# Turning the attention weights of slots 5 to 8 of the first batch on VectorE and through DRAM instead of on TensorE

## The chip, the cores and the metric

The kernel runs on one core of one Trainium2 chip. The metric is the device time of one execution in microseconds (us). Five engines work beside each other, each through its own instructions in order, and wait for one another by semaphores: TensorE (PE in the profile, with its weight loads PEld), VectorE (DVE), ScalarE (ACT), GpSimd (POOL) and SyncE (SP), whose queue issues nearly all DMAs here.

## The reference

For each of 8 batches and 8 heads, attention with a threshold: only the scores within tau of the row's maximum keep their weight. The heads of a batch are put side by side as x, and a feed-forward block (FFN) with normalisation follows.

```python
def _attn_ref(q, k, v, tau):              # q, k, v: (8, 8, 576, 64)
    scores = scale * np.matmul(q, k.transpose(0, 1, 3, 2))
    thresh = np.max(scores, axis=-1, keepdims=True) - tau
    scores = np.where(scores >= thresh, scores, -1000000000.0)
    scores = scores - np.max(scores, axis=-1, keepdims=True)
    attn = np.exp(scores)
    attn = attn / (np.sum(attn, axis=-1, keepdims=True) + 1e-09)
    return np.matmul(attn, v)

def _moe_ref(x, g_ln, w_ch1, w_ch2):      # x: (8, 576, 512); w_ch1: 512 x 2048, w_ch2: 2048 x 512
    mu = np.mean(x, axis=-1, keepdims=True)
    var = np.mean((x - mu) ** 2, axis=-1, keepdims=True)
    xn = (x - mu) / np.sqrt(var + 1e-06) * g_ln
    ch = np.maximum(xn @ w_ch1, 0.0) @ w_ch2
    return x + ch
```

The two weight matrices arrive as 64-bit floats; the kernel makes 32-bit floats of them on the chip.

## The kernel before

The kernel writes out the order of every engine's instructions by hand: what stands first in the Python code stands first in the engine's queue.

**Slots.** Attention goes through 72 slots, nine to a batch (`SLOTS`, with `HP` = 4 pairs of heads). Slots 0 to 3 take the first 256 queries of a pair of heads each, slot 4 takes the last 64 queries of all pairs together, slots 5 to 8 the second 256 queries. A slot has four quarters. In slot n, `scores` (matmuls on TensorE into PSUM) comes first; `exponentials` makes the negated maxima `neg` on VectorE (L372) and the exponentials `e` on ScalarE (L383); `weights` masks them and sums their rows on VectorE (L390) and takes the reciprocals `den` (L394). The scores of slot n+1 go into the same PSUM tiles, so they wait for L390 of slot n.

**Turning the weights.** For the product with v the weights must stand with the keys on the partitions. There are two ways, chosen by `by_blocks`. In batch 0, slot n+1 does it on TensorE (`turn_weights`): GpSimd makes four diagonal matrices of `den` (L404), and 36 matmuls of 64 columns by 128, that is four tiles `tp` and one tile `tr`, turn and divide at once; ScalarE copies each tile out of PSUM into `em` and `rest` (L437, L452). Two of the four tiles are turned ahead of the exponentials of slot n+1 and the others after the first two of them. In batches 1 to 7 `turn_blocks` does it: GpSimd divides `e` (L404), VectorE transposes blocks of 32x32 into `et` (L469), SP writes `et` to a DRAM buffer `scr` in four DMAs (L475), and in quarter 0 of the next slot `fetch` reads it back as `em` and `rest` in two (L484, L485). `values_of` multiplies with v (L511) in quarter 2 or 3 of slot n+1, ScalarE copies the result into `x`, and GpSimd sums x over its features (L537).

**The feed-forward part.** The 576 tokens of a batch make two groups of 288. When a group's last x is there, `mean_of` forms its mean by a matmul and `centre` subtracts it on VectorE (L552). `ffn_steps` yields 129 steps a group: first 16 tiles `hidden`, four matmul pairs each into one of two PSUM buffers with a relu on ScalarE (L606), and then 4 output tiles of 16 steps. `second_part` deals these steps out over the quarters: `ready(g)` names the quarter from which group g may run, and its steps are spread until `ready(g + 1)`.

**Weight chunks.** `Weights` brings the weights in 32 chunks of 128x512 64-bit numbers (16 of w_ch1, 16 of w_ch2), each into a piece of SBUF that is not yet needed for its own purpose (`w2_sb`, `hidden`, `et`, a tile `stage`). `fetch` issues the DMA on SP (L221), `tick` works on at most three chunks: `begin` (two VectorE and two ScalarE instructions), `carry` (GpSimd L257) one tick later, and `end` (VectorE L266, and GpSimd L271 for w_ch1) three ticks later. Slots 0 to 2 have three ticks each, slots 3 to 5 four, later ones six. A step of the feed-forward part whose weights are not made yet puts the quarter's work off.

Of the kernel before, what the change touches and what calls it, by code (L numbers as in the profile page):

```python
# [8 lines left out]
F32 = mybir.dt.float32  # L9
# [9 lines left out]
def kernel(  # L19
# [140 lines left out]
    class Weights:  # L160
# [12 lines left out]
        def __init__(self):  # L173
            self.chunks = [
                (w1_sb[i][:, c : c + WC], w_ch1[i * 128 : (i + 1) * 128, c : c + WC], i)
                for c in range(0, DF, WC)
                for i in range(NK)
            ] + [(w2_sb[:, i], w_ch2[i * 128 : (i + 1) * 128, :], None) for i in range(ND)]
            self.n1 = NK * (DF // WC)
            self.fetched = self.begun = self.carried = self.ended = 0  # L180
            self.raw, self.made, self.due, self.ticks = {}, {}, [], 2
            flat = lambda t: t.rearrange("p a b -> p (a b)")
            stage = consts.tile([128, 8, WC], F32, name="stage")
            et = att.tile([128, NB, 128], F32, tag="et", bufs=1, name="et0")

            n1 = self.n1
            self.free = []  # L190
            for t, n, before in (
                (w2_sb, ND // 2, lambda p: n1 + 2 * p),
                (hidden, 4, lambda p: 10),
                (et, 2, lambda p: 2 * n1),
                (stage, 4, lambda p: 2 * n1),
            ):
                for p in range(n):
                    self.free.append((before(p), -1, flat(t)[:, p * 2 * WC : (p + 1) * 2 * WC]))
# [84 lines left out]
            if self.begun < self.fetched:  # L283
                self.begin()

    def by_blocks(u):

        return units[u][0] > 0

    def turn(u):  # L290

        q_in, k_in = loaded.pop(u)
        qT = att.tile([128, 2, QH], F32, tag="qT", bufs=4, name="qT")
        kT = att.tile([128, S], F32, tag="kT", bufs=4, name="kT")
        qd = q_diag[u % HP]  # L300
        nc.gpsimd.tensor_scalar(
            out=q_in, in0=q_in, scalar1=scl_sb, scalar2=1.0, op0=ALU.mult, op1=ALU.mult
        )
        nc.vector.transpose(kT, k_in.rearrange("p n c -> p (n c)"))
        for s in range(2):
            part = q_in[:, 9 * s : 9 * s + 8]
            if by_blocks(u):
                nc.vector.transpose(
                    qT[:, s].rearrange("p (j a c) -> p a j c", j=2, a=4),
                    part.rearrange("p (a j) c -> p a j c", j=2),  # L310
                )
            else:
                nc.vector.transpose(qT[:, s], part.rearrange("p n c -> p (n c)"))
        for h in range(2):
            r = slice(64 * h, 64 * h + 64)
            nc.vector.transpose(
                qd[r, r].rearrange("p (t c) -> p t c", t=2),
                q_in[r].rearrange("p (t n) c -> p t n c", t=2)[:, :, 8],
            )
        turned[u] = (qT, kT, qd)  # L320
# [64 lines left out]
    def weights(es, thr, divide):  # L385


        den = small.tile([128, 4], F32, tag="den", name="den")
        for i in range(4):
            nc.vector.scalar_tensor_tensor(  # L390
                out=es[:, i], in0=blocks[i], scalar=thr[:, i : i + 1], in1=es[:, i],
                op0=ALU.is_ge, op1=ALU.mult, accum_out=den[:, i : i + 1],
            )
        nc.vector.reciprocal(den, den)  # L394
        diags = []
        for i in range(4):
            if divide:
                src = dst = es[:, i]
            else:
                if i % 2 == 0:  # L400
                    two = ffn.tile([128, TOK], F32, tag="o", bufs=6, name="diag")
                src, dst = ident, two[:, i % 2 * 128 : i % 2 * 128 + 128]
                diags.append(dst)
            nc.gpsimd.tensor_scalar(  # L404
                out=dst, in0=src, scalar1=den[:, i : i + 1], scalar2=1.0,
                op0=ALU.mult, op1=ALU.mult,
            )
        return diags
# [9 lines left out]
    def turn_weights(s, es, diags):  # L418


        em, er = turned_tiles(s)
        for i in range(4):
            if i == 2:
                yield
            tp = ps_ff.tile([128, J, 128], F32, tag="ff", name="tp")
            for c in range(J):
                product(
                    tp[:, c], lhsT=es[:, i, c * 128 : (c + 1) * 128], rhs=diags[i],
                    start=True, stop=True,
                )  # L430
            if s == HP:
                nc.scalar.copy(
                    em[:, :, :, 32 * i : 32 * i + 32], tp.rearrange("p c (a x) -> p c a x", a=4)
                )
            else:
                h, j = divmod(i, 2)
                nc.scalar.copy(  # L437
                    em[:, :, 2 * j : 2 * j + 2, 64 * h : 64 * h + 64],
                    tp.rearrange("p c (a x) -> p c a x", a=2),
                )  # L440
        tr = ps_ff.tile([64, 4, 128], F32, tag="ff", name="tr")
        for i in range(4):
            nc.tensor.matmul(  # L443
                tr[:, i], lhsT=es[:, i, J * 128 :], rhs=diags[i], start=True, stop=True
            )
        if s == HP:
            nc.scalar.copy(
                er[:64].rearrange("p a (u x) -> p u a x", u=HP),
                tr.rearrange("p u (a x) -> p u a x", a=4),
            )  # L450
        else:
            nc.scalar.copy(  # L452
                er[:64].rearrange("p a (h x) -> p h a x", h=2),
                tr.rearrange("p (h j) (a x) -> p h (j a) x", h=2, a=2),
            )
        yield em, er

    def turn_blocks(s, es):

# [35 lines left out]
    def values_of(b, s, turned_weights):  # L495

        em, er = turned_weights
        pv = pv_behind
        if b == 0 and s <= HP:
            pv = ps_ff.tile([128, QH], F32, tag="ff", name="pv")  # L500
        if s == HP:
            outs = [(hp, pv[:, hp * 64 : hp * 64 + 64]) for hp in range(HP)]
            pick = lambda t, hp, h: t[:, 2 * h : 2 * h + 2, hp * 32 : hp * 32 + 32]
        else:
            outs = [(s if s < HP else s - HP - 1, pv)]
            pick = lambda t, hp, h: t[:, :, 64 * h : 64 * h + 64]
        for hp, dst in outs:
            vt, vr = values_in[b * HP + hp]
            for c in range(J + 1):
                for h in range(2):  # L510
                    nc.tensor.matmul(  # L511
                        dst[64 * h : 64 * h + 64],
                        lhsT=vt[:, c, h, :] if c < J else vr[:, h, :],
                        rhs=pick(em[:, c] if c < J else er, hp, h),
                        start=(c == 0), stop=(c == J),
                    )
        if s == HP:
            for t in range(2):
                nc.scalar.copy(
                    x_of(2 * b + t)[:, :, QH:],  # L520
                    pv.rearrange("p (u t x) -> p t u x", u=HP, t=2)[:, t],
                )
                for c in range(1, NK):
                    add_feature(2 * b + t, c, slice(QH, TOK))
        else:
            g = 2 * b + (s > HP)
            hp = outs[0][0]
            nc.scalar.copy(x_of(g)[:, hp, :QH], pv)  # L528
            if hp:
                add_feature(g, hp, slice(0, QH))  # L530
# [114 lines left out]
    def at_quarter(n, i, fn, *args):  # L645
        later_calls.setdefault((n, i), []).append((fn, args))
# [5 lines left out]
    def ready(g):  # L652

        if g < 2:
            return (24, 41)[g]
        b, t = divmod(g, 2)
        return QUARTERS * (b * SLOTS + (HP, 2 * HP)[t] + 2) + (2, 4)[t]

# [43 lines left out]
    for n in range(NS):  # L702
# [24 lines left out]
        tick(1)  # L727
        run(n, 1)
        second_part(n, 1)
        blocks_go = by_blocks(b * HP)  # L730
        diags = weights(es, thr, blocks_go)
        run_all(aside)
        run_all(stores)
# [5 lines left out]
        if blocks_go:  # L739
            scr = turn_blocks(s, es)  # L740
            at_quarter(n + 1, 0, lambda s=s, scr=scr, box=box: box.append(fetch(s, scr)))
        else:
            made = turn_weights(s, es, diags)
            at_quarter(n + 1, -1, next, made)
            at_quarter(n + 1, 0, lambda made=made, box=box: box.append(next(made)))
        at_quarter(
            n + 1, 2 if b == 0 and s <= HP else 3,
            lambda b=b, s=s, box=box: values_of(b, s, box[0]),
        )
        if s in (HP, 2 * HP):  # L750
# [49 lines left out]
```

## Time and profile before

| | |
|---|---|
| median of 3 runs | 1514.7 us (1514.58 to 1514.93) |
| the profiled execution | 1510.16 us, span 1508.4 us |
| TensorE busy | 1423.0 us, 94% of the span |
| VectorE, ScalarE, GpSimd busy | 55%, 29%, 31% of the span |
| start of the scores of slots 0 to 5 | 9.6, 25.6, 39.6, 54.9, 69.8, 88.9 us |
| start of the scores of slots 6 to 10 | 113.7, 142.1, 170.2, 187.9, 221.1 us |
| first feed-forward matmul | 124.1 us |

The span is what the profiler saw of the kernel's own instructions; the profiled execution took 1.8 us more than it. Times in the timeline count from the span's start. A matmul in 32-bit floats is recorded as two records, and `product` issues two matmuls, so one feed-forward step leaves four records.

### The profile page before, as it was taken

What the parts mean: (1) busy time and instruction counts of PE and PEld (TensorE: products, weight loads), DVE (VectorE), ACT (ScalarE), POOL (GpSimd) and SP (SyncE); (2) the same over time, 40 slices, a digit from 0 to 9 for tenths busy, and PEclk for the clock granted to TensorE, in tenths of its full rate; (3) what the DMA queues carried; (4) which work ended last, traced back from release to release, by engine and by line L of the source; (5) the groups of instructions that cost most, each with busy time, mean ns of one, the idle gap of its engine ahead of it and who ended that gap; (6) DMA issues with size and microseconds to landing.
All of it is one profiled execution on the core that took longest, in us unless ns stands there. A gap on an engine that the chain in (4) does not pass through costs nothing.

```text
span 1508.4 us, 29807 instructions
## 1 busy us (share of the span) xinstructions
PE 1423.0 (94%) x12168; PEld 861.2 (57%) x12168; DVE 822.3 (55%) x1380; ACT 442.6 (29%) x797; POOL 470.5 (31%) x737
## 2 busy tenths in 40 slices
PE   4859999999999999999999999999999999999998
PEld 2647655565556555565556555565555655565554
DVE  5877646555645555455655556455564556455210
ACT  3655513223231322223132322314132232313120
POOL 3785323332323333232322323232232323232100
PEclk8879999999999999999999999999999999999999
DMA  9613146557765577456764577456774568545300
GB/s 226 164 56 107 38 98 140 161 138 163 167 159 132 133 160 173 128 138 153 172 168 120 133 167 175 131 138 155 169 170 129 139 150 185 138 114 132 95 9 16
DMA packets 460696, 205.12 MB, mean 136 GB/s; under 512 B 275024, under 2 KB 420176, under 8 KB 460560
## 3 DMA queue, kind: packets, MB, share of 16 engines
q1 hardware_dynamic: 458160, 202.93, 55.5%
q8 instruction: 95, 1.56, 0.4%
q10 hardware_dynamic: 2368, 0.30, 0.2%
q14 instruction: 41, 0.34, 0.1%
q0 software_dynamic: 32, 0.00, 0.0%
HBM read 119.41 MB, written 83.76 MB: 135 GB/s over the span
## 4 chain that ended last, share of the span: by engine, by line
PE 85%; ACT 6%; DVE 4%; SPq 1%; issue 1%; POOL 1%; DMA 1%; POOLq 0%; ACTq 0%; DVEq 0%
PE p L100 62%; PE sc L511 10%; PE sc L359 9%; ACT e L383 4%; DVE neg L372 2%; PE sc L100 2%; SPq L112 1%; ACT hidden L606 1%; PE tp L100 1%; DMA v_rest<-in_v_dram 1%; POOL diag L404 1%; PE tr L443 1%; ACT L383 1%; PE mean L100 1%; DVE e L390 0%
## 5 line engine op out<-in xcount | busy, mean ns | idle before, releaser
L100 PE MATMUL p<-xc,w 128*64 128x288 f32 x4096 | 520.6, 409 | 24.7 <-ACT hidden L606 24.1
L100 PE MATMUL p<-hidden,w 128*64 128x288 f32 x4096 | 513.6, 407 | 0.2 <-ACT rest L452 0.2
L100 PEld LDWEIGHTS p<-xc,w 128*64 128x64 f32 x4096 | 296.2, 137 | 227.5 <-ACT hidden L606 39.9
L100 PEld LDWEIGHTS p<-hidden,w 128*64 128x64 f32 x4096 | 293.3, 137 | 195.5 <-ACT rest L452 0.7
L372 DVE TENSOR_REDUCE neg<-sc 128x2 f32<-128x1152 f32 x144 | 189.4, 1353 | 343.5 <-PE sc L359 278.6
L383 ACT ACTIVATE e<-sc,neg 128x576 f32<-128x576 f32 x288 | 193.0, 743 | 275.8 <-DVE neg L372 275.6
L404 POOL TENSOR_SCALAR e<-e,den 128x576 f32<-128x576 f32 x252 | 183.6, 746 | 231.3 <-DVE den L394 226.4
L390 DVE SCALAR_TENSOR_TENSOR e<-sc,thr,e 128x576 f32<-128x576 f32 x288 | 219.1, 813 | 20.1 <-ACT e L383 19.4
L469 DVE STREAM_TRANSPOSE et<-e 128x1152 f32<-128x1152 f32 x112 | 153.2, 1372 | 72.8 <-POOL e L404 61.8
L359 PE MATMUL sc<-kT,qT 64*128 64x64 f32 (+3 forms) x1024 | 159.5, 445 | 27.0 <-DVE e L390 16.8
L606 ACT ACTIVATE hidden<-p 128x288 f32<-128x288 f32 x256 | 105.1, 415 | 270.3 <-PE p L100 268.3
L376 POOL TENSOR_SCALAR thr<-neg,low_sb 128x2 f32<-128x2 f32 x144 | 42.1, 293 | 374.6 <-DVE neg L372 371.6
L359 PEld LDWEIGHTS sc<-kT,qT 64*128 64x128 f32 x1024 | 88.8, 194 | 113.2 <-issue 81.5
L511 PE MATMUL sc<-em,v_in 128*64 128x256 f32 (+1 forms) x1408 | 130.8, 329 | 1.8 <-DVE o L569 1.8
L528 ACT COPY x<-sc 128x256 f32<-128x256 f32 x60 | 22.4, 373 | 321.5 <-PE sc L511 321.5
L511 PEld LDWEIGHTS sc<-em,v_in 128*64 128x64 f32 x1408 | 86.1, 137 | 40.3 <-DVE o L569 2.3
L569 DVE TENSOR_TENSOR o<-p,rb 128x288 f32<-128x288 f32 x64 | 28.4, 444 | 127.0 <-PE p L100 127.0
L570 POOL TENSOR_TENSOR o<-o,x 128x288 f32<-128x288 f32 x64 | 51.1, 798 | 137.3 <-DVE o L569 135.8
L537 POOL TENSOR_TENSOR sum<-sum,x 128x256 f32<-128x256 f32 (+1 forms) x64 | 31.4, 491 | 100.4 <-ACT x L528 97.9
L612 POOL TENSOR_TENSOR sq<-sq 128x288 f32<-128x288 f32 x48 | 39.0, 813 | 50.4 <-ACT sq L610 47.9
L618 DVE RECIPROCAL rb<-rb 128x288 f32<-128x288 f32 x16 | 31.2, 1950 | 35.3 <-ACT rb L617 35.0
L511 PE MATMUL sc<-rest,v_rest 128*64 128x256 f32 (+1 forms) x352 | 44.5, 329 | 0.0
(109 smaller groups left out, 741.2 us busy)
## 6 DMA issues: line engine op xcount, KB each, us to landing
scr<-et SPq DMA_DIRECT2D x252, 288.0 KB, 4.8
em<-scr SPq DMA_DIRECT2D x63, 1024.0 KB, 5.9
q_in<-in_q_dram SPq DMA_DIRECT2D x128, 72.0 KB, 3.7
out_dram<-ot SPq DMA_DIRECT2D x256, 36.0 KB, 4.1
k_in<-in_k_dram SPq DMA_DIRECT2D x124, 72.0 KB, 2.6
v_in<-in_v_dram SPq DMA_DIRECT2D x64, 128.0 KB, 4.1
rest<-scr SPq DMA_DIRECT2D x63, 128.0 KB, 6.0
w<-in_moe_w_ch_dram SPq DMA_DIRECT2D x12, 512.0 KB, 4.9
```

Source lines behind the costliest of these rows:

```text
L100: nc.tensor.matmul(out[r], lhsT=lhsT[:, r], rhs=rhs, **flags)
L359: nc.tensor.matmul(sc[h][:, at : at + n], lhsT=qT[r, half, j * 128 : (j + 1) * 128], rhs=kT[r, o : o + n], start=True, stop=True,)
L372: nc.vector.tensor_reduce(out=neg[:, i], in_=sc[h][:, : 2 * S].rearrange("p (j n) -> p j n", j=2), axis=AXL.X, op=ALU.max, negate=True,)
L376: nc.gpsimd.tensor_scalar(out=thr[:, i], in0=neg[:, i], scalar1=-1.0, scalar2=low_sb, op0=ALU.mult, op1=ALU.add,)
L383: nc.scalar.activation(es[:, i], blocks[i], func=AF.Exp, bias=neg[:, i : i + 1])
L390: nc.vector.scalar_tensor_tensor(out=es[:, i], in0=blocks[i], scalar=thr[:, i : i + 1], in1=es[:, i], op0=ALU.is_ge, op1=ALU.mult, accum_o ...
L404: nc.gpsimd.tensor_scalar(out=dst, in0=src, scalar1=den[:, i : i + 1], scalar2=1.0, op0=ALU.mult, op1=ALU.mult,)
L469: nc.vector.transpose(et[:, :, 64 * h : 64 * h + 64].rearrange("p n (j c) -> p j n c", j=2), es[:, 2 * h : 2 * h + 2].rearrange("p j (n c) ...
L511: nc.tensor.matmul(dst[64 * h : 64 * h + 64], lhsT=vt[:, c, h, :] if c < J else vr[:, h, :], rhs=pick(em[:, c] if c < J else er, hp, h), s ...
L570: nc.gpsimd.tensor_tensor(out=o, in0=o, in1=groups[g][:, m], op=ALU.add)
L606: nc.scalar.activation(hidden[:, d], p1, func=AF.Relu)
L612: nc.gpsimd.tensor_tensor(out=sq[:, 0], in0=sq[:, 0], in1=sq[:, c], op=ALU.add)
```

## The change

Five edits go together.

1. `by_blocks` now depends on the slot: in batch 0, slots 5 to 8 go by blocks and DRAM as all slots of later batches do. Their queries are transposed accordingly in `turn`.
2. The diagonals that are left (slots 0 to 4) are made by ScalarE, not by GpSimd.
3. `turn_weights` is no longer cut in two: all five tiles are turned ahead of the exponentials of slot n+1.
4. `ready` of the first two groups moves by a quarter. The mean of group 0 goes from the end of slot 5 to quarter 0 of slot 6, behind that slot's scores; the first feed-forward steps go from quarter 0 to quarter 1 of slot 6.
5. Pieces for chunks: those in `hidden` serve longer (up to chunk 15 to 18, before up to 9), those in `et` shorter (up to chunk 15, before to the end), and one tile `x_room` of the pool of x comes in.

```diff
@@ class Weights
             for t, n, before in (
                 (w2_sb, ND // 2, lambda p: n1 + 2 * p),
-                (hidden, 4, lambda p: 10),
-                (et, 2, lambda p: 2 * n1),
+                (hidden, 4, lambda p: n1 + p),
+                (et, 2, lambda p: n1),
+                (ffn.tile([128, NK, TOK], F32, tag="x", bufs=3, name="x_room"), 1, lambda p: 2 * n1),
                 (stage, 4, lambda p: 2 * n1),
             ):
@@
-    def by_blocks(u):
-
-        return units[u][0] > 0
+    def by_blocks(b, s):
+
+        return b > 0 or s > HP
@@ turn
-            if by_blocks(u):
+            if by_blocks(units[u][0], 2 * HP * s):
@@ weights
         for i in range(4):
-            if divide:
-                src = dst = es[:, i]
-            else:
+            if not divide:
                 if i % 2 == 0:
                     two = ffn.tile([128, TOK], F32, tag="o", bufs=6, name="diag")
-                src, dst = ident, two[:, i % 2 * 128 : i % 2 * 128 + 128]
-                diags.append(dst)
+                diags.append(two[:, i % 2 * 128 : i % 2 * 128 + 128])
+                nc.scalar.mul(diags[i], ident, den[:, i : i + 1])
+                continue
             nc.gpsimd.tensor_scalar(
-                out=dst, in0=src, scalar1=den[:, i : i + 1], scalar2=1.0,
+                out=es[:, i], in0=es[:, i], scalar1=den[:, i : i + 1], scalar2=1.0,
                 op0=ALU.mult, op1=ALU.mult,
             )
@@ turn_weights
         for i in range(4):
-            if i == 2:
-                yield
             tp = ps_ff.tile([128, J, 128], F32, tag="ff", name="tp")
...
-        yield em, er
+        return em, er
@@ values_of
-        if b == 0 and s <= HP:
+        if not by_blocks(b, s):
             pv = ps_ff.tile([128, QH], F32, tag="ff", name="pv")
@@ ready
         if g < 2:
-            return (24, 41)[g]
+            return (25, 42)[g]
@@ the loop over slots
-        blocks_go = by_blocks(b * HP)
+        blocks_go = by_blocks(b, s)
         diags = weights(es, thr, blocks_go)
...
         else:
-            made = turn_weights(s, es, diags)
-            at_quarter(n + 1, -1, next, made)
-            at_quarter(n + 1, 0, lambda made=made, box=box: box.append(next(made)))
+            at_quarter(
+                n + 1, -1,
+                lambda s=s, es=es, diags=diags, box=box: box.append(turn_weights(s, es, diags)),
+            )
         at_quarter(
-            n + 1, 2 if b == 0 and s <= HP else 3,
+            n + 1, 3 if blocks_go else 2,
             lambda b=b, s=s, box=box: values_of(b, s, box[0]),
         )
```

## The prediction

> **What bounds the kernel now.** I began with the page's forty slices of the span:
>
> ```profile
> PE   4859999999999999999999999999999999999998
> POOL 3785323332323333232322323232232323232100
> PEclk8879999999999999999999999999999999999999
> ```
>
> TensorE is full from the fourth slice (113 us) on; the idle time is ahead of it. Busy time slot by slot is the next view (columns: length, then busy time of PE, PEld, DVE, ACT, POOL; clock; DMA share; GB/s):
>
> ```profile
> 69.80:88.90 19.10, 13.65 (x127) 10.23 (x123) 15.61 (x29) 12.24 (x22) 14.71 (x15) 0.82 0.20 71
> 88.90:113.60 24.70, 13.21 (x173) 10.87 (x172) 17.09 (x29) 14.23 (x27) 21.84 (x28) 0.77 0.15 47
> 113.60:142.10 28.50, 25.81 (x238) 21.71 (x237) 24.51 (x35) 13.29 (x24) 15.54 (x16) 0.96 0.24 80
> 142.10:170.20 28.10, 25.74 (x241) 16.87 (x240) 17.17 (x27) 16.43 (x29) 9.05 (x11) 1.00 0.25 81
> 187.90:221.10 33.20, 29.96 (x274) 18.75 (x274) 12.69 (x24) 5.84 (x10) 8.02 (x12) 1.00 0.36 74
> 221.10:239.90 18.80, 18.80 (x156) 10.96 (x154) 12.49 (x24) 5.71 (x10) 7.33 (x11) 1.00 0.56 122
> ```
>
> Slots 4 and 5 are bound by a chain over VectorE, GpSimd and ScalarE; from slot 6 on TensorE sets the length, and what it is spared there shortens the run. Its timeline from slot 5 to slot 7 and in slot 9 (start, length, work, idle time before it):
>
> ```profile
> 112.49 1.23 PE L100 MATMUL mean<-sum,avg_sb 128*64 128x288 f32 x4 [6.33 <-POOL sum L537]
> 113.65 3.38 PE L359 MATMUL sc<-kT,qT 64*128 64x512 f32 x16
> 116.96 3.75 PE L100 MATMUL tp<-diag,e 128*64 128x128 f32 x64
> 123.40 0.98 PE L443 MATMUL tr<-diag,e 128*64 128x128 f32 x7 [2.69 <-ACT em L437]
> ...
> 124.33 12.29 PE L100 MATMUL p<-xc,w 128*64 128x288 f32 x99
> ...
> 144.35 3.89 PE L100 MATMUL tp<-diag,e 128*64 128x128 f32 x64
> 148.76 0.98 PE L443 MATMUL tr<-diag,e 128*64 128x128 f32 x7 [0.51 <-ACT em L437]
> ```
>
> The mean holds up the scores of slot 6 for 6.33 us, and each turn stands in front of feed-forward work. In the waits of slots 2 to 5 and in VectorE's timeline GpSimd is what is late: the diagonals, four in 3.5 us, stand ahead of the chunk work that VectorE needs next.
>
> ```profile
> 89.00 3.51 POOL L404 TENSOR_SCALAR diag<-ident,den 128x128 f32<-128x128 f32 x4 [2.44 <-PE pv L511]
> ```
> ```profile
> 50.06 0.77 DVE L313 STREAM_TRANSPOSE qT<-q_in 128x256 f32<-128x256 f32 x2 [2.15 <-POOL q_in L301]
> 77.34 1.20 DVE L266 SCALAR_TENSOR_TENSOR hidden<-hidden 128x512 f32<-128x512 f32 x1 [2.20 <-POOL hidden L257]
> 94.48 1.20 DVE L266 SCALAR_TENSOR_TENSOR et<-et 128x512 f32<-128x512 f32 x1 [2.20 <-POOL et L257]
> ```
>
> And the DMA prices (KB each, us from issue to landing):
>
> ```profile
> scr<-et SPq DMA_DIRECT2D x252, 288.0 KB, 4.8
> em<-scr SPq DMA_DIRECT2D x63, 1024.0 KB, 5.9
> w<-in_moe_w_ch_dram SPq DMA_DIRECT2D x12, 512.0 KB, 4.9
> ```
>
> **What the Trainium skill says.** "SBUF — State Buffer", section "SBUF: two separate sides": VectorE and GpSimd share one pair of ports under an exclusive lock, ScalarE never waits on it. The trace agrees: L266 takes 0.66 us beside an idle GpSimd and 1.20 us in the lines above. "DMA: Bandwidth & Descriptors", section "Two DMAs through the same engine are not ordered": a dependent DMA must wait at the issuing engine for the first one's semaphore. So SP itself stands still between `scr` and `em`; in slot 12 `scr` is issued at 271.25 us, takes 3.80 us, and `em` goes out at 279.04, 7.8 us after the first. "TensorE: Matmul & The Clock Gate", section "What's actually happening": an idle array falls to half clock and needs some 3.4 us to recover. After the 5.45 us gap of slot 4 `tr` takes 1.76 us instead of 0.98 and `pv` 3.62 instead of 1.89, some 2 us in all.
>
> **The change part by part.** All against the span of 1508.4 us.
>
> *Diagonals to ScalarE.* Slots 0 to 4 lose 3.5 us of GpSimd each. ScalarE pays four times 0.27 us (its 128x128 copy, the nearest row), about 1.1, and its two later ticks now queue behind `den`. VectorE's waits above go: in slot 2 the 2.15 us shrinks to some 0.5 (gain 1.65), and slots 3 and 4 gain 2.2 each plus about 1.2 from faster L266 and L243.
>
> *All five tiles ahead of the exponentials.* In slots 1 to 3 the last two exponentials end as before, within 0.8 us, since `rest` had been ahead of them anyway. In slots 4 and 5 it helps: `rest` sat at 85.10 between the halves because its tile waited 5.45 us for a copy behind the exponentials. With the copies done earlier I count the end of the exponentials of slot 4 at 82.0 instead of 86.9. Together with the diagonals: `den` of slot 4 at 83.8 instead of 88.7, that of slot 5 at 97.4 instead of 105.9. Early gain 8.5 us. Bounds: 3 if the ScalarE queue eats most of it, 11.
>
> *The first mean.* Scores of slot 6 start right after `den` of slot 5 (call that zero). But nothing then covers the mean: GpSimd divides `e` (4 x 0.73), does two chunk instructions (2.0) and six sums (1.8), so the sum is there at 7. VectorE has two ticks (3.6), the two transposes (2.75), two more ticks (3.6), `neg` (2.6), and only then `centre`: feed-forward starts at 14.1, where before it started at 18.2 (124.1 less 105.9).
>
> *The turns.* Removed from TensorE with their waits: 7.4 (slot 6, 116.96 to 124.33), 5.2 (slot 7), 5.2 (slot 8) and 8.2 (slot 9, where a tile at a time waits for its copy): 26 us. ScalarE loses 2.9 us a slot; VectorE gains two transposes (L469, 1372 ns each), GpSimd four divisions (L404, 2.91 us for four at 203.02), SP six DMAs. VectorE then needs some 21 us in slots 6 and 7, more than TensorE's 17 to 21, so it sets the length there.
>
> *SP and the chunks.* This is the new wait. The last seven chunks (26 to 32 in order) are fetched behind the new DMAs on SP. In the built order the 27th is issued after the `scr` of slot 6 and begun in that slot's last tick, ahead of the next `neg` on VectorE: 3.8 us of issue plus 4.9 to land, less 2.5 of other work, stops VectorE for about 6 us. The exponentials, and behind them the relus, wait for that `neg`; two PSUM buffers fill and TensorE stops 6.4 us in slot 7. The 30th chunk does the same over slots 7 and 8, and ScalarE's instruction for the 31st, which is behind the `em` of slot 7, stands in front of a relu: 6.7 us more. Add 0.8 for a smaller wait and 3 for the clock after gaps. The values themselves are hidden: `em` lands 13.8 us after the transposes, for slot 5 at 20 after zero, and is wanted at 23.
>
> *Room for chunks.* Nothing early: ticks limit the work, and 22 chunks are begun before the `neg` of slot 6 as before. Later one piece fewer is free, which is why chunk 27 comes late.
>
> *Sum.* From `den` of slot 5 I count slot lengths on TensorE: scores of slot 7 at 28, 8 at 57, 9 at 79, 10 at 100, and 102 with the clock. That is 97.4 + 102 = 199.4 instead of 221.05, with 111 feed-forward steps done instead of 120; the nine cost 0.49 us each (15.74 us for 128 records), 4.4. From slot 16 both orders are equal (272 steps each). Gain 21.65 - 4.4 = 17 us, all in a stretch after which TensorE is full. Span 1491, execution 1493; the median of the runs shown lies 4.5 us above the profiled execution, so 1497.5 on its scale.
>
> **The rivals.**
>
> A. The chunks are in time, since landing takes 3.2 us at best and VectorE may run later than I count. The 14 us of stalls and 3 of clock are saved: gain about 33, 1482. For it: before, no VectorE wait on a chunk is to be seen. Against it: the order on SP.
>
> B. ScalarE eats the early gain: diagonals, copies and conversion work in one queue ahead of the exponentials. Slots 0 to 5 gain only 3: 17 less 5.5, 1503. ScalarE is 14.2 of 24.7 us busy in slot 5, which speaks against it.
>
> C. Slower. Each of the seven chunks behind a round trip stops TensorE on its own, since `neg`, the exponentials and the relus are all behind chunk work. Seven times 6.5 is 45 us against savings of 33 without stalls: 1526. It decides from 4.8 us a chunk (33 over 7). Against it: three or four of the seven are issued in pairs or have a whole tick's slack.
>
> D. No change: the removed turns were filled idle time, and the end is set elsewhere. Against it: TensorE is busy 18.80 of 18.80 us in slot 10. 1514.
>
> **How the numbers follow.** Main case 0.55, A 0.17, B 0.15, C 0.09, D 0.04. A difference within 0.2%, 3 us, can't be told from no change. Faster: main, A and B, 0.87; same: D, 0.04; slower: C, 0.09. The main case alone spans 1488 to 1504 (early gain 3 to 11, stalls 10 to 20). The range, 1483 to 1508, takes in most of A and all of B and leaves C and D out.
>
> **What would show it.** Right: scores of slot 6 at about 98 us and ahead of the mean; first feed-forward matmul near 111; no `tp` after it; VectorE idle some 6 us before L241 (the chunk's first instruction) on a chunk's DMA near 127 to 133 us; TensorE gaps of 6 us ended by a relu in slots 7 and 8; scores of slot 10 near 199; equal slot lengths from slot 16. Wrong: chunk waits absent (A), `den` of slot 5 past 102 (B), gaps in more than three places (C), or `values_of` waiting for `em`.

## The result: no difference, and the profile after

The changed kernel takes 1514.76 us (median of 4 runs, 1513.69 to 1515.84), the kernel before 1514.64 us in the same comparison: ratio 1.0003, 95% interval 0.9986 to 1.002. The forecast was 1497.5 us and a gain.

The profiled execution took 1514.96 us, with a span of 1513.2 us, 4.8 more than the span before. The medians do not differ by that much: the profiled execution of before lay 4.5 us below its median, that of after on it. So the traces tell where time went inside two executions, and the medians tell that the sum is nothing. Early starts also differ between executions of the same instructions: the kernel with edit 4 alone, below, is the kernel before up to `den` of slot 5, and reached it at 107.20 us, the trace of before at 105.78.

The forty slices after:

```profile
PE   4766699999999999999999999999999999999998
...
POOL 2585333232323233232322323232331323222100
PEclk9888899999999999999999999999999999999999
```

TensorE's first four slices are no fuller than before (4, 7, 6, 6 for 4, 8, 5, 9), and the fifth is down to 6. Slot by slot (length, then busy time of PE, PEld, DVE, ACT, POOL; clock; DMA share; GB/s), from the start of slot 4's scores to that of slot 11's:

```profile
72.40:88.60 16.20, 10.89 (x124) 7.45 (x124) 16.03 (x24) 12.10 (x24) 12.00 (x11) 1.00 0.31 106
88.60:104.80 16.20, 13.71 (x168) 10.81 (x168) 16.03 (x24) 11.92 (x23) 12.19 (x12) 0.79 0.11 34
104.80:139.80 35.00, 21.58 (x136) 12.31 (x136) 31.95 (x46) 13.92 (x27) 23.57 (x28) 0.71 0.30 83
139.80:171.20 31.40, 22.80 (x172) 14.10 (x170) 21.10 (x28) 12.46 (x23) 13.82 (x13) 0.89 0.50 139
171.20:199.50 28.30, 17.25 (x125) 9.49 (x124) 17.35 (x28) 8.86 (x15) 8.77 (x10) 0.82 0.65 166
199.50:220.10 20.60, 20.59 (x171) 12.12 (x169) 11.96 (x22) 3.01 (x5) 7.20 (x11) 1.00 0.84 168
```

Slots 4 and 5 are bound by VectorE (16.03 busy of 16.20 us): GpSimd is no longer what is late, as forecast, but VectorE is busy as long as before (32.1 us in the two slots for 32.7). Slots 6 to 8 have 13.4, 8.6 and 11.1 us in which TensorE does nothing. Only in slot 9 is TensorE full without the turn (20.6 us instead of 33.2, where the turn had 8.2). The scores of slot 10 start at 220.1 us, before at 221.05, with nine feed-forward steps fewer behind them; at the 0.49 us a step of the prediction that is 3.5 us behind the kernel before. TensorE's timeline (start, length, work, idle time before it and what ended it):

```profile
114.44 1.23 PE L100 MATMUL mean<-sum,avg_sb 128*64 128x288 f32 x4 [4.25 <-POOL sum L536]
124.46 10.84 PE L100 MATMUL p<-xc,w 128*64 128x288 f32 x76 [8.80 <-DVE xc L551]
...
154.50 3.90 PE L100 MATMUL p<-xc,w 128*64 128x288 f32 x16 [8.32 <-ACT hidden L605]
...
188.57 8.30 PE L100 MATMUL p<-hidden,w 128*64 128x288 f32 x52 [11.05 <-ACT hidden L605]
```

No `tp` stands between these any more. There are four waits instead, 32.4 us in all. VectorE's timeline has the other side of the last two, and two early lines:

```profile
70.78 0.82 DVE L392 SCALAR_TENSOR_TENSOR e<-sc,thr,e 128x576 f32<-128x576 f32 x1 [2.53 <-ACT e L385]
...
75.99 1.79 DVE L268 SCALAR_TENSOR_TENSOR w<-w 128x512 f32<-128x512 f32 x1
...
149.72 0.43 DVE L241 TENSOR_SCALAR stage<-stage 128x512 uint32<-128x512 uint32 x1 [5.73 <-DMA stage<-in_moe_w_ch_dram]
...
180.64 0.43 DVE L241 TENSOR_SCALAR stage<-w 128x512 uint32<-128x512 uint32 x1 [11.52 <-DMA w<-in_moe_w_ch_dram]
```

The first two lines are early. One is a wait for exponentials; the forecast did not count on it, though before had one of 1.93 us in the same slot. The other is L268 (L266 before) at 1.79 us, where its free run is 0.66. GpSimd's side of it:

```profile
75.50 1.73 POOL L259 TENSOR_TENSOR hidden<-hidden,w 128x512 int32<-128x512 int32 x1
```

GpSimd's addition starts 0.49 us ahead of L268 and ends at 77.23 us; L268 ends at 77.78, 0.55 later. So L268 stood still behind the addition for most of its 1.79 us. The last two lines of VectorE are the chunk waits. On SP the chunk of the last line stands behind the four writes:

```profile
168.05 3.82 SPq L474 DMA_DIRECT2D scr<-et  x4
171.98 1.43 SPq L223 DMA_DIRECT2D w<-in_moe_w_ch_dram  x1
```

Issued at 171.98, it was there when VectorE went on at 180.64, 8.7 us later. The medians are less, 5.7 us over all chunks (KB each, us from issue to landing):

```profile
scr<-et SPq DMA_DIRECT2D x268, 288.0 KB, 4.8
w<-in_moe_w_ch_dram SPq DMA_DIRECT2D x14, 512.0 KB, 4.7
stage<-in_moe_w_ch_dram SPq DMA_DIRECT2D x8, 512.0 KB, 6.5
```

### The profile page after: what moved, and what is told of

The parts are those of the page before. It is cut to its first block, busy times and chain, and to the rows that moved or that the text cites. A ratio compares the mean times of both kernels' runs of the same rounds, so it can differ in the third digit from the quotient of the medians.

```text
span 1513.2 us, 29229 instructions
## 1 busy us (share of the span) xinstructions
PE 1413.2 (93%) x11880; PEld 840.3 (56%) x11880; DVE 842.1 (56%) x1388; ACT 437.8 (29%) x797; POOL 464.6 (31%) x717
## 4 chain that ended last, share of the span: by engine, by line
PE 80%; DVE 6%; ACT 4%; SPq 3%; DMA 3%; issue 2%; POOL 1%; POOLq 0%; ACTq 0%; DVEq 0%
PE p L100 59%; PE sc L510 9%; PE sc L361 9%; ACT e L385 3%; DVE neg L374 2%; PE sc L100 2%; SPq L112 2%; DMA stage<-in_moe_w_ch_dram 1%; DVE e L392 1%; ACT hidden L605 1%; SPq L474 1%; PE tp L100 1%; DVE w L268 1%; PE mean L100 0%; POOL e L405 0%
## 5 line engine op out<-in xcount | busy, mean ns | idle before, releaser
L405 POOL TENSOR_SCALAR e<-e,den 128x576 f32<-128x576 f32 x268 | 198.3, 757 | 248.6 <-DVE den L396 235.7
L468 DVE STREAM_TRANSPOSE et<-e 128x1152 f32<-128x1152 f32 x120 | 164.0, 1372 | 76.7 <-POOL e L405 55.0
L361 PE MATMUL sc<-kT,qT 64*128 64x448 f32 (+3 forms) x1024 | 165.1, 451 | 33.9 <-DVE e L392 24.4
```

The source lines that it names most:

```text
L361: nc.tensor.matmul(sc[h][:, at : at + n], lhsT=qT[r, half, j * 128 : (j + 1) * 128], rhs=kT[r, o : o + n], start=True, stop=True,)
L405: nc.gpsimd.tensor_scalar(out=es[:, i], in0=es[:, i], scalar1=den[:, i : i + 1], scalar2=1.0, op0=ALU.mult, op1=ALU.mult,)
L468: nc.vector.transpose(et[:, :, 64 * h : 64 * h + 64].rearrange("p n (j c) -> p j n c", j=2), es[:, 2 * h : 2 * h + 2].rearrange("p j (n c) ...
```

## The experiments

Two theories stood against each other at first. **Chunks:** the turns' time was won, and lost again to chunk fetches behind the new DMAs on SP. **Early part:** the early gain is missing, for a reason that lies on VectorE, ScalarE or GpSimd. Ratios are to the kernel before, with 95% intervals; the kernel before had medians of 1513.7 to 1514.0 us beside these runs. Times within a slot come from one profiled execution of each version.

### Chunk fetches first

```diff
@@ the loop over slots
-        run(n, 0)
         conversion.fetch(2)
+        run(n, 0)
...
+        conversion.fetch(2)
         box = []
         if blocks_go:
             scr = turn_blocks(s, es)
...
         run_all(aside)
-        conversion.fetch(2)
         run(n, 3)
```

> All of the change, but chunk DMAs are issued on SP ahead of the scr writes and ahead of the read-back em instead of behind them; nothing else moves. Theory (the chunks come late because SP issues them behind the DRAM round trip): VectorE's waits of 5.73, 2.32 and 11.52 us before L241 shrink to under 1 us each, TensorE's gaps of 8.32 and 11.05 us in slots 7 and 8 go, and the run is 15 to 19 us faster than the change, 1496 to 1500 us. Rival (chunks are late because the DMA engines are full with scr and em, or the work between is VectorE's anyway): waits stay over 3 us each, gain under 5 us, 1510 to 1515.

1504.23 us, ratio 0.9944 (0.9929 to 0.9959). VectorE's timeline:

```profile
149.36 0.43 DVE L241 TENSOR_SCALAR stage<-stage 128x512 uint32<-128x512 uint32 x1 [0.74 <-DMA stage<-in_moe_w_ch_dram]
174.94 0.43 DVE L241 TENSOR_SCALAR stage<-stage 128x512 uint32<-128x512 uint32 x1 [2.01 <-DMA stage<-in_moe_w_ch_dram]
```

The chunk waits of 5.73 and 11.52 us are down to 0.74 and 2.01, TensorE's of 8.32 and 11.05 to 2.77 and 5.35. The 27th chunk goes out at 122.16 us instead of 143.44, the 30th at 148.65 instead of 171.98. So behind `scr` the fetches had waited for more than its 3.8 us of issue: SP issues in order, and the writes themselves wait for VectorE's transposes (33.5 us in two waits of SP in the changed kernel, between 120 and 182 us). The order on SP is a cause, worth 9 us by the ratios (10.5 by the medians) and not the 15 to 19 expected; the 31st chunk still goes out behind four loads of v, at 171.16 us.

### The turn in two parts again

```diff
@@ turn_weights
         for i in range(4):
+            if i == 2:
+                yield
...
-        return em, er
+        yield em, er
@@ the loop over slots
-            at_quarter(n + 1, -1, lambda ...: box.append(turn_weights(s, es, diags)))
+            made = turn_weights(s, es, diags)
+            at_quarter(n + 1, -1, next, made)
+            at_quarter(n + 1, 0, lambda made=made, box=box: box.append(next(made)))
```

> All of the change, but turn_weights is cut in two again (two tiles ahead of the exponentials, the others behind the first two). Theory (turning all five tiles first delays the exponentials of slots 1 and 3, where VectorE now waits 1.56 and 2.53 us for ScalarE): the scores of slot 4 start about 3 us earlier than with the change (72.4), but slots 4 and 5 become longer again (before: 19.2 and 24.7 us, change: 16.2 and 16.2), so the scores of slot 6 come later than 104.8, at 106 to 109; the run within 3 us of the change. Rival (the cut is what cost the early gain): slot 6 at 100 or earlier and the run 4 us faster or more.

1517.85 us, 1.0021 (1.0007 to 1.0035): slower than the kernel before; that it is 3 us slower than the changed kernel is not clear of noise, since that one's interval reaches 1.002. Slot 4 starts earlier (68.54 for 72.40), but slots 4 and 5 take longer: in each, `tr` waits 4.5 us for a copy behind the exponentials, and slot 6 starts at 106.21 instead of 104.82. So edit 3 pays in slots 4 and 5. That it costs anything in slots 1 to 3 isn't shown: in this trace TensorE ran the scores of slot 3 at full clock, in that of the changed kernel at half (see "TensorE kept busy"), and with edits 2 and 3 alone, below, slot 4 starts at 67.75 us with the turn in one piece.

### The diagonals on GpSimd again

```diff
@@ weights
-                nc.scalar.mul(diags[i], ident, den[:, i : i + 1])
+                nc.gpsimd.tensor_scalar(out=diags[i], in0=ident, scalar1=den[:, i : i + 1], scalar2=1.0,
+                                        op0=ALU.mult, op1=ALU.mult)
```

> All of the change, but the diagonals of slots 0 to 4 are made by GpSimd again. Theory (moving them brought nothing, because GpSimd's chunk work then falls on VectorE's two-input instructions and the port is locked): VectorE's L268 falls from 1.78 us back to about 0.7 after den, a wait of 2.2 us for GpSimd returns, and the scores of slot 6 start within 2 us of 104.8; the run within 3 us of the change. Rival (the move is worth what was predicted, and something else ate it): slot 6 starts 4 to 6 us later and the run is that much slower.

1513.91 us, 0.9997 (0.9987 to 1.0007), slot 6 at 104.84 us. VectorE waits for GpSimd again:

```profile
79.95 1.20 DVE L268 SCALAR_TENSOR_TENSOR hidden<-hidden 128x512 f32<-128x512 f32 x1 [2.20 <-POOL hidden L259]
96.03 1.21 DVE L268 SCALAR_TENSOR_TENSOR w<-w 128x512 f32<-128x512 f32 x1 [2.20 <-POOL w L259]
```

But each line is 0.58 us shorter than its counterpart in the changed kernel, and so are others: L268 takes 11.9 us in all between 39 and 106 us, with the diagonals on ScalarE 16.1. Here edit 2 trades a wait for longer instructions and no gain is seen.

### The first mean as before

```diff
@@ ready
-            return (25, 42)[g]
+            return (24, 41)[g]
```

> All of the change, but the mean of the first group is again ahead of the scores of slot 6, and the feed-forward part begins a quarter earlier. Theory (with blocks, VectorE's queue between den of slot 5 and neg of slot 6 is 15 us long, so putting the mean behind the scores leaves TensorE 8.8 us without cover while the scores didn't need to be early): centre comes right behind the transposes, the first feed-forward matmul starts at 116 to 119 us instead of 124.5, and the scores of slot 7 come no later although slot 6 holds 32 steps instead of 24; gain at slot 7 at equal work 3 to 6 us, of which the chunk waits of slots 7 and 8 take most: run 0 to 5 us faster than the change. Rival (the late mean helps): first matmul no earlier, run slower by 3 us or more.

1509.89 us, 0.9979 (0.9969 to 0.9989): 4.9 us better than the changed kernel by the medians, 3.6 by the ratios. The mean waits 10.47 us ahead of the scores of slot 6, and the first feed-forward matmul still comes earlier, at 118.60 us instead of 124.46: `centre` is not behind the chunk work of the slot. 1.3 of the 5.9 us is from `den` of slot 5, which was at 105.02 here although the instructions up to it are those of the changed kernel (106.28). The trace has a new kind of wait later: TensorE reaches weights that aren't made, 4.82 us up to its matmul at 184.10.

### GpSimd's addition left out

```diff
@@ carry
-            nc.gpsimd.tensor_tensor(out=ai, in0=ai, in1=self.words(i, I32)[:, :, 0], op=ALU.add)
```

The weights lose the last three bits of the mantissa.

> All of the change, but carry's GpSimd addition (L259) is left out, so the weights lose the last three bits of their mantissa; the ScalarE instruction that feeds it stays. Theory (the early gain failed because GpSimd's two-input additions, no longer held back by the diagonals, run at the same time as VectorE's L268 and L245 and lock the port they share): L268 falls from 1.1 to 1.3 us to 0.7 on the mean of slots 2 to 5, the way from den of slot 4 to neg of slot 5 from 8.9 us to under 6.5, and the scores of slot 6 start at 97 to 100 us, about where the prediction had them (98), instead of 104.8. Rival (the chain of copies, exponentials and slow TensorE clock sets the early slots): slot 6 not before 103.

1507.61 us, 0.9961 (0.9951 to 0.9972). The lines that were L268 (L267 here) take 0.66 to 0.69 us in all slots up to 5, so it is the collision with GpSimd's addition that makes them long. Slot 4 is 14.01 us long instead of 16.23. But then VectorE runs into the next limit:

```profile
101.06 0.82 DVE L391 SCALAR_TENSOR_TENSOR e<-sc,thr,e 128x576 f32<-128x576 f32 x1 [2.43 <-ACT e L384]
```

Slot 6 starts at 102.68, between what theory (97 to 100) and rival (103 or later) gave: a shorter VectorE waits for exponentials.

### Edit 1 alone, and with edit 5

```diff
--- before
-                (et, 2, lambda p: 2 * n1),
+                (et, 2, lambda p: n1),
@@
-        return units[u][0] > 0
+        return b > 0 or s > HP
...
-            n + 1, 2 if b == 0 and s <= HP else 3,
+            n + 1, 3 if blocks_go else 2,
```

> The kernel before with the first edit alone: slots 5 to 8 turned by blocks and through DRAM, diagonals on GpSimd, turning cut in two, the first mean where it was; of the chunk pieces only those in et end at chunk 15, as they must. Theory (26 us of TensorE work are saved and chunk waits of VectorE behind the DRAM round trip take most of it): slots 0 to 4 as before, VectorE waits on chunk DMAs in slots 6 to 8 of 10 to 20 us in all, run between 1503 and 1512 us. Rival (the DRAM way itself costs nothing and the other four edits ate the gain): no VectorE wait on chunks over 2 us, run under 1497 us.

1534.75 us, 1.0136 (1.0112 to 1.016): slower by 21 us, which no theory had. Its VectorE and TensorE timelines:

```profile
148.60 0.43 DVE L239 TENSOR_SCALAR stage<-w 128x512 uint32<-128x512 uint32 x1 [9.15 <-DMA w<-in_moe_w_ch_dram]
179.98 0.43 DVE L239 TENSOR_SCALAR stage<-stage 128x512 uint32<-128x512 uint32 x1 [8.82 <-DMA stage<-in_moe_w_ch_dram]
208.10 0.43 DVE L239 TENSOR_SCALAR stage<-stage 128x512 uint32<-128x512 uint32 x1 [10.73 <-DMA stage<-in_moe_w_ch_dram]
```

```profile
217.50 1.23 PE L100 MATMUL p<-hidden,w 128*64 128x288 f32 x4 [15.95 <-DVE w L266]
```

With fewer pieces the last fetches are issued a slot later (201.30 us, with edit 5's pieces at 178.94); three stop VectorE, and at 217.50 TensorE has waited 15.95 us for a weight. Two more took this apart. The first puts edit 5's pieces on top:

```diff
-                (hidden, 4, lambda p: 10),
+                (hidden, 4, lambda p: n1 + p),
+                (ffn.tile([128, NK, TOK], F32, tag="x", bufs=3, name="x_room"), 1, lambda p: 2 * n1),
```

> The kernel before with edits 1 and 5 (blocks and DRAM, with the whole new set of pieces). Theory: without the pieces the conversion ran behind the feed-forward steps, which cost 20 us; with them it is a slot earlier, the TensorE gap of 16 us in slot 9 that waits for a weight is gone, and the time is 1513 to 1522. Rival: pieces were not what was short there, the order of the chunk fetches on SP behind scr alone was: the gaps stay, 1530 or more.

1513.69 us, 1.001 (0.9999 to 1.0021). The gap of 15.95 us is gone, and two chunk waits stay (6.23 and 9.22 us, in an execution that was the slowest of 20, 1519.74 us). So beside edit 1, edit 5 is worth 21 us. The second leaves the few pieces as they are and moves the fetches, as in the first experiment:

> The kernel before with edit 1 alone, and the chunk fetches ahead of the four scr writes and of the read-back on SP. Theory: fetches behind scr are a cause also there: VectorE's waits for chunks (9.2, 8.8 and 10.7 us with edit 1 alone) fall under 3 us each and the time to 1515 to 1525. Rival: with so few pieces a fetch cannot be issued earlier, whatever its place on SP: waits and gaps stay, 1531 or more.

1507.24 us, 0.9954 (0.9939 to 0.9969): 27.5 us better than edit 1 alone, and 6.5 better than the kernel before. One chunk wait is left, of 0.94 us. That the turns off TensorE are worth something is shown here. But only 6.5 us of the 26 come through; of the rest, 12.7 us (3.03, 7.13 and 2.52) stand in the trace as waits of TensorE for weights that VectorE has not made:

```profile
188.66 1.23 PE L100 MATMUL p<-hidden,w 128*64 128x288 f32 x4 [7.13 <-DVE w L266]
```

### Edit 4 alone

The line of "The first mean as before" the other way round, on the kernel before.

> The kernel before with edit 4 alone (first mean behind the scores of slot 6, first feed-forward steps a quarter later). Theory: the scores of slot 6 start some 6 us earlier, near 107.5, but the steps start no earlier than before (124 us) since centre waits behind VectorE's chunk work, so that the time is within 3 us of before. Rival A: a mean behind the scores is worse, as it was in the changed kernel, by about 5 us: 1519. Rival B: the earlier scores let the following slots run earlier: 1508 or less.

1514.32 us, 0.9999 (0.999 to 1.0008). The scores of slot 6 start at 106.34 instead of 113.65, and by slot 10 that is gone (220.77 and 221.05). Neither rival held: on its own edit 4 does nothing.

### Edits 2 and 3 alone, and with edit 5

The edits are those of the change, on the kernel before.

> The kernel before with edits 2 and 3 alone (diagonals on ScalarE, the turn in one piece); TensorE still turns slots 5 to 8. Theory: the early part gains nothing, because GpSimd's chunk additions now collide with VectorE's and VectorE waits for late exponentials: scores of slot 6 at 112 to 115 us (before 113.7), time within 3 us of before. Rival: the two edits do give an early gain, which the other three edits hid: scores of slot 6 at 106 or earlier, time 1508 or less.

1508.31 us, 0.9963 (0.995 to 0.9976). The rival was right: `den` of slot 5 is at 101.64 us, before at 105.78, after at 106.28. There is an early gain of 4.1 us when these two edits stand alone, with L266 at 1.78 us as in the changed kernel. So collisions on VectorE aren't what separates the two, though they keep the gain below 8.5. The one difference among VectorE's waits is that those for `e` of 1.56 and 2.53 us (slots 1 and 3) are missing, 4.1 of the 4.6 us. Against the kernel before, 1.84 us of the 4.1 are gained in slots 4 and 5 and most of the rest in slot 3, where before had a wait of 1.93 us for `e`. Of the other edits, 4 acts from slot 6 on and 1 changes only two transposes in `turn` that early. TensorE's clock and edit 5 were tried next; edit 1's transposes were not tried apart.

> The kernel before with edits 2, 3 and 5. Theory (the clock, not the pieces): the early slots are as in e9 or a little later, as the clock falls; scores of slot 5 at 84 to 87, time 1508 to 1512. Rival (pieces): scores of slot 5 at 88 or later and the time back at 1513 or more.

1508.59 us, 0.9956 (0.994 to 0.9972), `den` of slot 5 at 101.67: edit 5, on its own beside these two, takes nothing from the early slots.

### TensorE kept busy

In slot 3 of the changed kernel the scores start after 4.21 us of idle time and take 5.89 us, and the turn behind them 5.37. Busy time and clock there, in steps of 1 us:

```profile
63.00:64.00 1.00, 1.00 (x14) 1.00 (x12) 1.00 (x2) 0.00 (x0) 1.00 (x2) 0.50 1.02 414
64.00:65.00 1.00, 1.00 (x14) 1.00 (x12) 1.00 (x2) 0.38 (x1) 1.00 (x1) 0.50 0.85 340
65.00:66.00 1.00, 1.00 (x14) 1.00 (x12) 1.00 (x2) 0.20 (x1) 0.43 (x2) 0.55 0.09 33
66.00:68.00 2.00, 2.00 (x39) 1.92 (x34) 1.97 (x4) 1.22 (x3) 1.34 (x2) 1.00 0.82 254
```

The clock is at half (0.50; 14 records a us) until 65.9 us, 9 us after the scores began. Because the whole turn now stands in front of the exponentials on ScalarE, its slowness goes straight to VectorE. The trace of before has the same slow slot 3, with less of the turn in front of the exponentials:

```profile
54.89 5.90 PE L359 MATMUL sc<-kT,qT 64*128 64x512 f32 x16 [3.74 <-DVE e L390]
60.71 5.60 PE L100 MATMUL tp<-diag,e 128*64 128x128 f32 x64
```

VectorE waited there for `e` 1.93 us in slot 3 and not at all in slot 1; after the change 2.53 and 1.56. The test fills the idle time:

```diff
         run(n, 3)
+        if n < 3:
+            keep = ps_ff.tile([128, 512], F32, tag="ff", name="keep")
+            for _ in range((12, 6, 6)[n]):
+                product(keep, lhsT=ident, rhs=turned[n][1][:, :512], start=True, stop=True)
         second_part(n, 3)
```

> The changed kernel with matmuls of no use (identity by kT, 128x512, into a PSUM tile that nobody reads) at the end of slots 0 to 2, twelve pairs and then six and six, so that TensorE isn't idle ahead of the scores. The result is unchanged. Theory (the clock): the scores of slots 1 and 3 take 3.4 us instead of 5.89, the turn after them 3.8 instead of 5.4, VectorE's waits for e in slots 1 and 3 (1.56 and 2.53 us) are gone, the scores of slot 5 start at 84 to 85 instead of 88.6, and the time falls by 3 to 5 us to about 1510. Rival (pieces, or the length of VectorE's own work): scores of slot 5 still at 88 or later, time 1513 to 1517.

```profile
52.09 5.32 PE L100 MATMUL keep<-kT,ident 128*64 128x512 f32 x24
57.34 2.33 PE L361 MATMUL sc<-kT,qT 64*128 64x512 f32 x16
59.60 3.81 PE L100 MATMUL tp<-diag,e 128*64 128x128 f32 x64
```

The scores of slot 3 now take 2.33 us, the turn 3.81, both waits for `e` are gone, `den` of slot 5 is at 101.93, and the span is 1508.5, 4.7 less. So in the profiled execution the clock was the cause. In the median less is seen: 1513.07 us, 0.9993 (0.9986 to 1.0001), with single runs from 1508.45 to 1515.54; the profiled one took 1510.35. How much an average execution loses this way stays open, between nothing and 5 us.

What decides where the clock is slow is open too. The page "TensorE: Matmul & The Clock Gate", section "What's actually happening", has the clock follow a free-running window, so that the cold stretch differs from run to run. The traces agree that it differs: the version with the first mean as before has the same instructions up to here, and in its slot 1 TensorE is at 24 records a us from 31 us on, in the changed kernel at 12 to 14 still from 32 to 35 us. But chance needn't be all of it. All eight traces of versions with edits 1 and 3 and without added matmuls have a wait of 2.0 us or more for `e` in slot 3; the two with edits 2 and 3 but not 1 have none. That edit 1 has a part in it was not tested.

### Faster than both

These are the changed kernel with fetches first and the mean as before, and then with the values of slot 4 a quarter earlier too, so that the sum for the mean comes sooner:

```diff
@@ the loop over slots
-            n + 1, 3 if blocks_go else 2,
+            n + 1, 3 if blocks_go else 1 if s == HP else 2,
```

> All of the change with two edits undone or mended: chunk DMAs ahead of the round trip, and the mean ahead of the scores of slot 6. Theory (the two losses are separate: 9.6 us in slots 6 to 8, 4 us in slot 6): they add, 1499 to 1502 us. Rival (with earlier feed-forward work the conversion of the weights is what TensorE waits for, as the gaps of 1.3 to 4.8 us ended by VectorE's L268 with the early mean say): 1503 to 1507 us, no better than the chunks alone.

> As the one before, and besides the values of slot 4 are formed in quarter 1 of slot 5 instead of quarter 2, so that GpSimd's sums stand ahead of its four divisions. Theory (the mean waits for GpSimd: division 4.96 us, then chunk work, then the sums): the mean matmul's wait falls from 10.5 us to under 4, scores of slot 6 start at 105 to 107 instead of 114.3, but centre still stands behind the transposes on VectorE, so the first feed-forward matmul is at 113 to 117 and the run 1 to 3 us faster than the one before. Rival: VectorE's queue decides alone, no difference over 1 us.

Without that last line 1500.41 us, 0.9902 (0.987 to 0.9933); with it 1498.51, 0.9897 (0.9876 to 0.9919). TensorE's timeline with it:

```profile
105.93 0.71 PE L100 MATMUL mean<-sum,avg_sb 128*64 128x288 f32 x4 [3.02 <-POOL sum L536]
...
115.56 6.59 PE L100 MATMUL p<-xc,w 128*64 128x288 f32 x32 [4.98 <-ACT stage L253]
```

The first feed-forward matmul is 9.3 us after `den` of slot 5 (106.26), in the changed kernel 18.2. Two variants of this version:

> The fastest version so far (e8) without edit 5's pieces: those in hidden up to chunk 9 only and no x_room, those in et up to chunk 15. Theory: with fetches ahead the conversion needs the room too, since edit 1 alone with fetches ahead still waited 7.1 us for a weight in slot 9: 1500 to 1508, slower than e8's 1498.5. Rival (edit 5's pieces cost the early slots 4 us and are not needed when fetches come first): 1492 to 1496.

1503.99 us, 0.993 (0.9917 to 0.9943), with slot 5 at 88.52 us, against 88.61 with the pieces: they cost nothing early, and are worth 5.5 us here.

> The fastest version so far (e8) with the matmuls of no use of e13. Theory (the clock): the early gain of 3 to 5 us carries through to the end, 1494 to 1496. Rival: no difference to e8, 1497 to 1500, since later chunk work takes the gain up.

1495.97 us, 0.9885 (0.987 to 0.99), the lowest median of all, though its interval overlaps that of the version without the added matmuls.

## Why the prediction was wrong

Slot 10 was forecast at 199.4 us and came at 220.1, 20.7 later: 8.9 up to `den` of slot 5 (106.28, not 97.4), and 11.8 from there on (113.8 us, not 102).

**Diagonals to ScalarE.** That VectorE's waits for GpSimd go was right. That L266 and L243 get faster (1.2 us a slot) was wrong, and it is the first failed term: GpSimd, rid of the diagonals, begins its two-input additions just ahead of VectorE's two-input instructions. In each of slots 4 and 5 two of the four L268 take 1.78 us, not 0.66, and most L245 1.06, not 0.69; in slot 4 VectorE's twelve chunk lines add up to 11.0 us, before to 8.6. The page "SBUF — State Buffer" of the Trainium skill, cited in the prediction for the lock between these engines, was applied to the old times only and not to the new ones, although the trace of before has one such line in slot 6:

```profile
137.37 1.77 DVE L266 SCALAR_TENSOR_TENSOR w<-w 128x512 f32<-128x512 f32 x1 [2.24 <-POOL w L257]
```

By the forecast slot 2 would get 1.65 us shorter and slots 4 and 5 (which turn slots 3 and 4, as the prediction calls them) 3.4 each, 8.5 in all. From `den` to `den`, slot 2 took 15.28 us before and after, and slots 4 and 5 went from 17.14 to 16.2: 1.9 in all. So this term is some 6.5 of the 8.9 us. Without GpSimd's addition slot 4 did take 14.0 us, near the 13.7 of the forecast; slot 5 then waited for exponentials.

**All five tiles ahead of the exponentials.** "The last two exponentials end as before" in slots 1 to 3 failed: VectorE waited 1.56 and 2.53 us for `e`, where before it waited 0 and 1.93, and `den` of slot 3 came 2.4 us later than before. That is about the rest of the 8.9. The whole turn, at half clock, now stood in front of the exponentials. The prediction priced the clock after gaps in later slots and left it out here, with 3.4 us to recover; measured are 5 and 9, and the trace of before had shown as much (half clock from 25.6 to 30.5 us in slot 1 and from 54.9 to 64.6 in slot 3). The 3.4 us are from the page "TensorE: Matmul & The Clock Gate"; the measurement decides. The rival that ScalarE eats the early gain named the right place, the row in front of the exponentials, and the wrong cause: ScalarE was not too busy, it waited for TensorE's tiles. Of the early gain of 8.5 us, minus 0.5 was left. Alone the two early edits gained 4.1 us, inside the bounds of 3 to 11, but about half of that came in slot 3, where TensorE ran at full clock in that trace; no term counted on this.

**The first mean.** 14.1 us to the first feed-forward matmul was 18.2, no shorter than before. The order of the steps was right. What failed were the durations, taken from engines that don't disturb each other: the four divisions took 4.96 us, not 2.91, and the sum came late with them (its mean waited 4.25); VectorE's ticks had lines of 1.65 (L245), 1.76 (L268) and 1.50 (L241), and `neg` started at 121.34, 15.1 us after `den`, where the steps of the forecast add up to 10.0.

```profile
106.64 4.96 POOL L405 TENSOR_SCALAR e<-e,den 128x576 f32<-128x576 f32 x4 [1.61 <-DVE den L396]
```

**The turns.** No `tp` or `tr` is left after slot 5, as costed. TensorE's busy time fell by 9.8 us only (1423.0 to 1413.2), less than four times 4.9 for these matmuls; that the others ran at clocks of 0.71 to 0.89 in slots 6 to 8 fits this. VectorE set the length of slot 6, as forecast, but with 30.5 us of work from `den` of slot 5 to the scores of slot 7, so that these came at 33.5 us after `den` and not at 28.

**SP and the chunks.** The mechanism was right: VectorE waited 5.73 us for the 27th chunk where 6 was forecast, in slot 6's last tick and ahead of `neg` (later than 127 to 133, since the slot ran to 139.8). Mis-sized were its effect on TensorE, 8.32 us for 6.4, and the second stop, 11.05 for 6.7: its chunk needed 8.7 us to land, not 4.9. It was issued right behind `scr` and ahead of four loads of v; which of these slowed it isn't shown. The rival of seven stops did not happen; three chunks stopped VectorE and two of these stops reached TensorE.

**Room for chunks.** "Nothing early" held. "One piece fewer, which is why chunk 27 comes late" counts the pieces rightly against the kernel before, but the cause was another: with the same pieces and the fetches first, this chunk went out 21 us earlier and VectorE did not wait for it. What the prediction did not see is what edit 5 is for: without its pieces edit 1 loses 21 us.

**Sum and rivals.** Of the 20.7 us, 8.9 were lost early, 4.1 at the mean, and 7.7 after it, where the two stops were 6.3 longer than counted (19.4 for 13.1). The median misses the forecast by less, 17.3 us, because the forecast took the traced execution to be 4.5 us faster than the median, and that of after was not. The rival of no change had the time right and the reason wrong: the removed turns were not idle time, most of what they took came back as waits.

## What to carry to other kernels

When an engine is relieved, ask what its remaining work will now run beside: a wait that vanishes between VectorE and GpSimd can return as longer instructions on both. A DMA that is moved onto a queue can delay what stands behind it: here the loads waited until the data of four writes was there and for the 3.8 us of their issue, and one of them then took 8.7 us to land where 5.7 is the median of all chunks. So put loads with a deadline ahead of round trips. And where the trace shows TensorE slow after idle time, price the next matmuls at that speed, and see who stands behind them.

## What the hardware showed beyond expectation

The lock costs as much as is left of the other engine's instruction: L268, 0.66 us alone, took 1.20 or 1.78, and in both cases ended some 0.55 us after the two-input instruction of GpSimd that had begun ahead of it (1.78 in the lines above; for 1.20 in the trace of before, GpSimd's L537 ended at 77.98 us and L266 at 78.54). After idle time TensorE worked 5 us at half clock in slot 1 of the trace of before and nearly 10 in slot 3, one and the same execution; what sets the length isn't shown.
